# Attention through landmarks followed by an MLP: other buffers, another order of loads, and queries by parity of heads

## The chip, the core and the metric

The kernel runs on one core of a Trainium2 chip. A core has TensorE (PE: matmuls; PEld: its weight loads), VectorE (DVE), ScalarE (ACT), GpSimd (POOL) and SyncE (SP), which work beside each other and wait for one another by semaphores, a store SBUF, and PSUM, into which TensorE writes. [...] The metric is the device time of one execution in microseconds; lower is better.

## The reference

For each of 8 batches and 8 heads, with 576 tokens of 64 values and 32 landmarks:

```python
p_packed = sm_attn(p, k, v)            # softmax(scale * p k^T) v  : 32 x 64 per head
out      = sm_attn(q, p_packed, p_packed)   # 576 x 64 per head
x = out.transpose(0, 2, 1, 3).reshape(8 * 576, 512)
h = x @ w_in                           # 512 -> 2048
g = where(h >= 1, h, where(h <= -1, 0, (h + 1) ** 2 / 4))
return g @ w_out                       # 2048 -> 512, float32
```

Inputs are float32 and are drawn at random; the output is 4608 x 512 float32.

## The kernel before

All heads of a batch are worked on together, in bf16. Head h is G*a + g with G = 2, so g is its parity and a its pair. For each batch:

- The loads `k`, `q`, `v` (96 partitions, 8 heads, 6 x 64) are issued by POOL, which casts. The first four heads of batch 0's k, and batch 0's landmarks (`p_raw`), come as float32 by SP's and ACT's queues and are cast afterwards. The other batches' landmarks are one POOL load.
- `turned` (batches 0 and 1): TensorE transposes k and q head by head into `tp` in PSUM (line 362), VectorE and ScalarE copy them to `kT` and `qT`. `crossed` (batches from `FIRST` = 2): a DMA transpose on SP does it.
- `landmarks`: TensorE transposes p (`tpp`, line 321), four copies bring it to `pT`.
- `scores`: `sp` = kT by pT (line 413), exponential to `ex` (line 419). `packed`: `pk` = v by ex, with sums (lines 445, 450), to `ppT` and the scales `rs`.
- `probs`: `s` = ppT by qT (line 472), one PSUM tile for each parity g. Then for each g: exponential `eT` (482), sums `sm` (487), `ln` (491), `rc` = exp(-ln) (495), and on VectorE `A` = eT * rs * rc (500).
- The packed values are not multiplied out: `M` = w_in by ppT (`mp`, line 528, in four parts of 512 columns; then a copy) takes the place of w_in.
- `hidden`: for each of 16 slices fi of 128 hidden units, `h` = M by A (562); ScalarE makes `x` (567); VectorE or ScalarE the cut `t` (572, 574); VectorE `hT` = min(t, 1) * t (579).
- `output`: two batches are 9 tiles of 128 tokens; each is 16 matmuls `o` (619) over fi, a copy to `ob` and a store by SP (637).

PSUM has a pool `w` of three double banks for everything but outputs, and two banks for `o`.

The order on every engine is written out by a planner when the program is built. Each step is a `Task` with a rank, a price on each engine that may do it, what it depends on and which buffers it takes. `Plan.run` places the steps one after another in time, by its own prices, and the kernel is emitted in that order; the chip then runs each engine's list in order, with waits. Ranks come from constants at the top (`H1`, `T1`, `EARLY` and so on). Loads are a chain in the order of the list `LOADS`, of which at most eight are under way; a load also waits until the buffer that it fills is free. `BUFS` gives one buffer each to k and q, two to v. Finally, where the planner leaves TensorE free before the first output matmul, `warm` puts matmuls of zeros ("fillers", line 687), so that its clock stays up:

```python
n = math.ceil((t.start - at) / 0.2135) if at < 5.0 else int((t.start - at - 0.1) / 0.1085)
...
for w in [FW] * (n // 2) + [FW // 2] * (n % 2):
    nc.tensor.matmul(o[:, :w], zeros[:, :P], zeros[:, :w], start=True, stop=True)
```

How many fillers there are is fixed when the program is built.

Of the kernel before, what the change touches and what calls it, by code (L numbers as in the profile page):

```python
# [116 lines left out]
def kernel(  # L117
# [11 lines left out]
    f32 = mybir.dt.float32  # L129
    bf16 = mybir.dt.bfloat16  # L130
# [3 lines left out]
    B, H, S, D = q.shape  # L134
# [21 lines left out]
    PITCH0, PITCH1 = 1.03, 0.66  # L156
    T1, T2 = 3.22, 22.00
    LENT = [1, 4, 8]
    L1, M1 = 11.28, 4.03
    KT1, QT1 = 7.75, 9.62  # L160
    SC1, PK1 = 10.75, 9.34
    ST1, MT1 = 13.56, 16.34
    EARLY = [[(3.51, 23.7), (10.45, 10.36), (23.64, 1.0), (31.73, 16.65)], [(32.99, 9.77), (42.87, 11.2), (54.6, 5.54), (55.23, 18.49), (57.85, 4.06)]]

    V, A_, G_ = nc.vector, nc.scalar, nc.gpsimd
    nc.scalar.preload_act_table_set("natural_log_exp_and_others")

    BUFS = dict(w=3, o=2, k=1, q=1, v=2, kT=2, qT=2, ex=2, ppT=2, M=2, A=2, eT=4, ln=2, rc=2, x=4, t=4, ob=4)
    const = ctx.enter_context(tc.tile_pool(name="const", bufs=1))
# [48 lines left out]
    def constants(e):  # L218
        V.memset(zeros, 0.0)  # L219
        V.memset(pT[:, 0].rearrange("p g a x n -> p (g a x n)"), 0.0)  # L220
# [6 lines left out]
    consts = plan.add(-1000, {"DVE": (2.2, 2.2, constants)})  # L227

# [13 lines left out]
    def dma(key, rank, emit, mb, takes=(), settle=0.9):  # L242
# [6 lines left out]
        return t  # L249

    def tokens(nm, b):
        if (nm, b) not in have:
            have[nm, b] = new(nm, [TP, H, NC, D], bf16)
        return have[nm, b].rearrange("p h c d -> p h (c d)")

    def rows_of(nm, b, h0, h1):
        return {"k": k, "q": q, "v": v}[nm][b, h0:h1].rearrange("h (p c) d -> p h (c d)", c=NC)

    def load(nm, b, rank):

        parts = {("k", 0): [4, 8], ("q", 0): [0, 4, 6, 8]}.get((nm, b), [0, 8])
        for i, (h0, h1) in enumerate(zip(parts, parts[1:])):
            def emit(e, h0=h0, h1=h1):
                G_.dma_start(tokens(nm, b)[:, h0:h1], rows_of(nm, b, h0, h1))  # L264
            mb = MB0.get((nm, b, h0), 1.18 * (h1 - h0) / H)
            t = dma((nm, b, h0), rank + 0.01 * i, emit, mb, [nm] if i == 0 else [], 0.9 if b < 3 else 3.0)
            for h in range(h0, h1):
                landed[nm, b, h] = [t]
# [8 lines left out]
    def load_p(rank):  # L277
        dma("p", rank, lambda e: G_.dma_start(p_nat[:, 1:].rearrange("n b h d -> n (b h) d"),
                                              p[1:].rearrange("b h n d -> n (b h) d")), 0.6)

# [13 lines left out]
    def load_p_raw(e):  # L294
        for i, queue in enumerate((nc.sync, nc.scalar)):
            queue.dma_start(p_raw[:, 4 * i:4 * i + 4], p[0, 4 * i:4 * i + 4].rearrange("h n d -> n h d"))

    p_first = plan.add(-1000, {"SP": (1.0, 3.3, load_p_raw)})

    def load_k_raw(e):  # L300
        for i, queue in enumerate((nc.sync, nc.scalar)):
            queue.dma_start(k_raw[:, 2 * i:2 * i + 2], rows_of("k", 0, 2 * i, 2 * i + 2))

# [32 lines left out]

    p_cast = plan.add(-900, {"DVE": (0.41, 0.41, lambda e: V.tensor_copy(p_nat[:, 0], p_raw))}, [p_first])
    landmarks(0, 1, -900, [p_cast, identity])

    A_of, M_of, rs_of = {}, {}, {}  # L340

    def attention(b, at, fine):

        ready = {}

        def turned(nm, h0, h1):

            n = h1 - h0
            rank = at[nm + "T"] + 0.075 * h0
            banks = [(0, (0, 2)), (1, (2, 3))] if n == 4 else [(j, (0, E)) for j in range(n)]  # L350

            def place(tp, j, c):
                return tp[:, 0, (j * 2 + c) * TP:][:, :TP] if n == 4 and c < 2 else \
                    tp[:, 1, j * TP:][:, :TP] if n == 4 else tp[:, j, c * TP:][:, :TP]

            def turn(e):
                if h0 == 0:
                    have[nm + "T", b] = new(nm + "T", [P, H, E, TP], bf16)
                have["tp" + nm, b, h0] = tp = wide([P, 2, 1024], bf16, "tp")
                for c in range(E):  # L360
                    for j in range(n):
                        nc.tensor.transpose(place(tp, j, c),  # L362
                                            have[nm, b][:, h0 + j, X * c:X * (c + 1)].rearrange("p c d -> p (c d)"),
                                            ident[:TP, :TP])

            t = plan.add(rank, {"PE": (0.51 * n / 4, 0.17 + 0.51 * n / 4, turn)}, landed[nm, b, h0] + [identity],
                         ["w"] + ([nm + "T"] if h0 == 0 else []), behind=[ready.get((nm, "turn"))])
            ready[nm, "turn"] = t
            ev = []
            for y, (c0, c1) in banks:  # L370
                to = lambda y=y, c0=c0, c1=c1: (have[nm + "T", b][:, h0:h1, c0:c1] if n == 4 else
                                                have[nm + "T", b][:, h0 + y])
# [8 lines left out]
            for h in range(h0, h1):  # L381
                ready[nm, h] = ev
            return t

        def crossed(nm):
            def turn(e):
                have[nm + "T", b] = T = new(nm + "T", [P, H, E, TP], bf16)
                nc.sync.dma_start_transpose(T.rearrange("p h e t -> p (h e) t"),
                                            have[nm, b].rearrange("p h c d -> p (h c d)"))
            t = plan.add(at[nm + "T"], {"SP": (3.5, 11.0 if b < 4 else 6.5, turn)}, landed[nm, b, 0], [nm + "T"])  # L390
            chain("crossed", t)
# [5 lines left out]
        for nm in "kq":  # L397
            parts = [0, 4, 6, 8] if (nm, b) == ("q", 0) else [0, 4, 8]
            users[nm] = [turned(nm, *p) for p in zip(parts, parts[1:])] if b < FIRST else crossed(nm)
            plan.release(nm, users[nm])  # L400

# [28 lines left out]
        if b == 0:  # L430
            have["others"] = plan.add(-27, {"DVE": (1.56, 1.56, lambda e: V.memset(
                pT[:, 1:].rearrange("p b g a x n -> p (b g a x n)"), 0.0))}, [consts], behind=ready["k", 4])

# [31 lines left out]

        def probs(e):
            for g in range(G):
                have["s2", b, g] = s2 = wide([P, X, FW], f32, "s2")
# [6 lines left out]

        s2 = plan.add(at["s2"], {"PE": (0.32, 0.47, probs)}, pp + list({id(t): t for h in range(H) for t in ready["q", h]}.values()), ["w", "w", "eT", "eT"], mode="s")
        plan.release("qT", [s2])
        before = None
        for g in range(G):
# [23 lines left out]
            r = at["sm"] + 0.2 * g  # L503
            t_e = plan.add(r, {"ACT": (0.68, 0.745, exp)}, [s2, rs])
            plan.release("w", [t_e])
# [13 lines left out]
        for fs in groups:  # L519
# [28 lines left out]
        plan.release("ppT", mms + [s2])  # L548

# [173 lines left out]
```

## Time and profile before

| what | value |
| --- | --- |
| median of 3 runs | 249.87 us (249.86 to 250.2) |
| the profiled execution | 250.52 us |
| its span, first to last instruction | 248.7 us |
| busy: PE, PEld | 239.0, 136.7 us |
| busy: DVE, ACT, POOL | 176.9, 194.2, 27.9 us |
| granted TensorE clock | 1.000 |

A row of the timeline gives start, time taken, engine, line, operation, what is written and read, the number of instructions that were merged, and in brackets idle time of the engine ahead of it with what ended that. Of rows "who waited for whom" the numbers are total, times and longest. A busy TensorE is not one at its peak, since ends of matmuls are modelled; the starts of neighbours tell its pace. "DMA to landing" counts from the start of the issuing instruction.

### The profile page before, as it was taken

How to read it: one execution, taken by the hardware profiler on the slowest of the kernel's cores; microseconds unless marked ns; L12 is line 12 of the kernel's file. 1: busy time of each engine (PE TensorE's matmuls, PEld its weight loads, DVE VectorE, ACT ScalarE, POOL GpSimd, SP SyncE). 2: the span in 40 equal slices, each digit the busy share in tenths (PEclk: the TensorE clock that was granted, in tenths of full speed). 3: DMA queues.
4: the chain of work that ended last, by engine and by line, in shares of the span. 5: the costliest groups of instructions: out<-in, count | busy, mean ns of one | idle time of the engine just before them, and what ended most of it. 6: DMA issues, size and time to landing. Idle time of an engine off the chain costs nothing.

```text
span 248.7 us, 5748 instructions
## 1 busy us (share of the span) xinstructions
PE 239.0 (96%) x2330; PEld 136.7 (55%) x2368; DVE 176.9 (71%) x294; ACT 194.2 (78%) x320; POOL 27.9 (11%) x41
## 2 busy tenths in 40 slices
PE   7999999999999999999999999999999999999993
PEld 2645665456555664664556455655564555555453
DVE  4549997469937998897976796878976676776000
ACT  3587896889878999989997988799668978886111
POOL 8542100300110030021003000300000000000000
PEclk9999999999999999999999999999999999999999
DMA  7999999399999999799997979894941111122223
GB/s 153 189 206 207 200 199 194 58 228 196 179 169 223 173 164 214 123 180 175 195 147 150 202 160 176 154 204 110 171 105 45 42 45 42 43 46 77 59 75 84
DMA packets 59179, 35.83 MB, mean 144 GB/s; under 512 B 31888, under 2 KB 54672, under 8 KB 59152
## 3 DMA queue, kind: packets, MB, share of 16 engines
q0 software_dynamic: 24496, 18.29, 50.2%
q1 hardware_dynamic: 34080, 16.65, 32.2%
q10 hardware_dynamic: 576, 0.52, 0.7%
q8 instruction: 18, 0.29, 0.5%
q14 instruction: 9, 0.07, 0.1%
HBM read 37.22 MB, written 9.44 MB: 188 GB/s over the span
## 4 chain that ended last, share of the span: by engine, by line
PE 81%; DMA 8%; DVE 4%; ACT 2%; issue 2%; POOL 1%; POOLq 0%
PE o L619 44%; PE h L562 22%; DMA kT<-k 5%; DMA q<-in_q_dram 3%; PE mp L528 3%; DVE hT L579 2%; PE pk L445 2%; PE sp L413 2%; PE o L687 2%; PE sm L487 2%; PE s L472 1%; PE tp L362 1%; DVE t L572 1%; PE pk L450 1%; ACT x L567 1%
## 5 line engine op out<-in xcount | busy, mean ns | idle before, releaser
L619 PE MATMUL o<-w_out_sb,hT 128*128 128x512 bf16 (+1 forms) x557 | 142.3, 373 | 2.1 <-issue 0.5
L579 DVE SCALAR_TENSOR_TENSOR hT<-t 128x576 bf16<-128x576 f32 x128 | 95.1, 756 | 13.6 <-ACT t L574 11.1
L567 ACT ACTIVATE x<-h 128x576 f32<-128x576 f32 x128 | 80.3, 657 | 14.5 <-PE h L562 12.4
L562 PE MATMUL h<-A,M 128*128 128x288 bf16 x512 | 80.8, 286 | 0.8 <-DVE A L500 0.3
L619 PEld LDWEIGHTS <-hT 128*128 128x128 bf16 x592 | 56.0, 98 | 46.3 <-issue 4.5
L562 PEld LDWEIGHTS <-M 128*128 128x128 bf16 x512 | 49.4, 98 | 31.2 <-issue 2.6
L572 DVE TENSOR_SCALAR t<-x 128x576 f32<-128x576 f32 x72 | 33.6, 467 | 10.7 <-ACT x L567 10.2
L574 ACT ACTIVATE t<-x 128x576 f32<-128x576 f32 x56 | 38.5, 690 | 1.0
L189 ACT COPY ob<-o 128x512 f32<-128x512 f32 (+1 forms) x21 | 11.9, 568 | 15.7 <-PE o L619 15.7
L189 DVE CAST M<-mp 128x1024 bf16<-128x1024 f32 (+1 forms) x14 | 16.6, 1183 | 8.3 <-PE mp L528 8.2
L189 ACT CAST M<-mp 128x1024 bf16<-128x1024 f32 (+1 forms) x19 | 18.5, 994 | 2.2 <-PE mp L528 2.2
L264 POOL DMA_DIRECT2D q<-in_q_dram x10 | 7.3, 735 | 105.8 <-DMA qT<-q 82.0
L500 DVE SCALAR_TENSOR_TENSOR A<-eT,rs,rc 128x576 bf16<-128x576 bf16 x16 | 12.3, 812 | 3.5 <-ACT rc L495 3.5
L189 DVE COPY ob<-o 128x512 f32<-128x512 f32 x16 | 11.0, 689 | 5.3 <-PE o L619 4.8
L419 ACT ACTIVATE ex<-sp 96x768 bf16<-96x768 f32 x16 | 12.1, 801 | 2.9 <-PE sp L413 2.9
L687 PE MATMUL o<-zeros 128*128 128x512 bf16 (+1 forms) x45 | 12.6, 398 | 1.4 <-DVE zeros L219 1.2
L482 ACT ACTIVATE eT<-s,rs 128x576 bf16<-128x576 f32 x16 | 11.0, 737 | 1.0 <-DVE t L572 0.5
L491 ACT ACTIVATE ln<-sm 128x576 f32<-128x576 f32 x16 | 10.3, 652 | 0.5 <-PE sm L487 0.2
L189 ACT CAST ppT<-pk 64x128 bf16<-64x128 f32 x18 | 4.7, 259 | 7.6 <-PE pk L450 7.3
L528 PE MATMUL mp<-w_in_sb,ppT 64*32 64x512 bf16 x256 | 10.4, 382 | 0.0
L495 ACT ACTIVATE rc<-ln 128x576 f32<-128x576 f32 x16 | 10.0, 679 | 0.0
L413 PEld LDWEIGHTS <-kT 128*128 128x128 bf16 x192 | 7.3, 100 | 3.2 <-DMA kT<-k 0.7
(47 smaller groups left out, 108.5 us busy)
## 6 DMA issues: line engine op xcount, KB each, us to landing
v<-in_v_dram POOLq DMA_DIRECT2D x8, 576.0 KB, 10.0
out_dram<-ob SPq DMA_DIRECT2D x23, 192.0 KB, 2.4
k<-in_k_dram POOLq DMA_DIRECT2D x7, 576.0 KB, 11.9
q<-in_q_dram POOLq DMA_DIRECT2D x7, 576.0 KB, 6.9
out_dram<-ob SPq DMA_DIRECT2D x24, 128.0 KB, 2.4
w_in_sb<-in_moe_w_in_dram POOLq DMA_DIRECT2D x4, 512.0 KB, 13.1
w_out_sb<-in_moe_w_out_dram POOLq DMA_DIRECT2D x4, 512.0 KB, 18.3
out_dram<-ob SPq DMA_DIRECT2D x23, 64.0 KB, 2.0
```

The source lines that it names most:

```text
L189: i = (nc.vector.tensor_copy if e == "DVE" else nc.scalar.copy)(to, of)
L413: nc.tensor.matmul(o, kT[:, j * TP:j * TP + w], pT[:, b, g, 2 * i + a], start=True, stop=True)
L419: nc.scalar.activation(have["ex", b][:, :, 64 * i:64 * i + 64], have["sp", b, i][:TP, :E * X * G], AF.Exp, scale=scale)
L500: V.scalar_tensor_tensor(have["A", b][:, g], have["eT", b, g], rs_of[b][:, g, :1], have["rc", b, g], ALU.mult, ALU.mult)
L528: nc.tensor.matmul(mp[a * NP:(a + 1) * NP, g], have["ppT", b][r, g, a], w_in_sb[r, a, f * FW:(f + 1) * FW], start=True, stop=True)
L562: nc.tensor.matmul(h[:, hf, :HALF], M[:, g, fi * P:(fi + 1) * P], A[:, g, hf], start=(g == 0), stop=(g == G - 1))
L567: nc.scalar.activation(x, have["h", b, fi][:, :, :HALF], AF.Prelu, bias=-1.0, alpha=0.5)
L572: V.tensor_scalar(t, have["x", b, fi], 1.0, 0.0, ALU.add, ALU.max)
L574: nc.scalar.activation(t, have["x", b, fi], AF.Relu, bias=1.0)
L579: V.scalar_tensor_tensor(dst, t, 1.0, t, ALU.min, ALU.mult)
L619: nc.tensor.matmul(have["o", key][:, :w], hT[:, fi, i * P:(i + 1) * P], w_out_sb[:, fi, cols], start=(fi == 0), stop=(fi == KF - 1))
L687: nc.tensor.matmul(o[:, :w], zeros[:, :P], zeros[:, :w], start=True, stop=True)
```

## The change

It has four parts, and the planner's constants are set anew with them.

1. Batch 1's q gets a buffer of its own, `q1`, in the place of `k_raw`, which is free once batch 0's k has been cast; `p_raw` becomes a tile named `k1`, used by it alone. Batch 2's q then needs only batch 0's q to be transposed.
2. `LOADS`: batch 1's v comes ahead of the last two parts of w_out, the landmarks move behind batch 1's q, w_out's first part ahead of w_in's third, batch 2's v ahead of its q and k.
3. Batch 0's q is loaded and transposed in three parts by parity: heads 0 2 4 6, then 1 3, then 5 7 (before: 0 to 3, 4 5, 6 7). `probs` is two steps in batch 0, one for each parity, so the even half needs only the first part. Which engine makes the copies of the first part is fixed, and so is ScalarE for the first half of M's first part.
4. Landmarks of batches 0 and 1 come together by SP's and ACT's queues (one batch each) and are transposed together; the POOL load has six batches instead of seven, and their transposes come at batch 2's rank.

```diff
-    LOADS = "k0 v0 q0 win0 win1 win2 wout0 win3 wout1 k1 p wout2 v1 wout3 q1 q2 k2 v2"
-    H1, H2 = 18.20, 43.17
-    T1, T2 = 3.22, 22.00
+    Q0 = [range(0, 8, 2), range(1, 5, 2), range(5, 9, 2)]
+    LOADS = "k0 v0 q0 win0 win1 wout0 win2 win3 wout1 k1 v1 wout2 wout3 q1 v2 p q2 k2"
+    H1, H2 = 20.58, 43.72
+    T1, T2 = 1.70, 16.92
...
-    BUFS = dict(w=3, o=2, k=1, q=1, v=2, ...)
+    BUFS = dict(w=3, o=2, k=1, q=1, q1=1, v=2, ...)
...
-    p_raw = const.tile([NP, H, D], f32, name="p_raw")
+    p_raw = work.tile([NP, 2, H, D], f32, tag="k1", name="p_raw", bufs=1)
-    k_raw = const.tile([TP, 4, NC * D], f32, name="k_raw")
+    k_raw = work.tile([TP, 4, NC * D], f32, tag="q1", name="k_raw", bufs=1)
...
+    def home(nm, b):
+        return "q1" if (nm, b) == ("q", 1) else nm
...
-            queue.dma_start(p_raw[:, 4 * i:4 * i + 4], p[0, 4 * i:4 * i + 4].rearrange("h n d -> n h d"))
+            queue.dma_start(p_raw[:, i], p[i].rearrange("h n d -> n h d"))
...
-    landmarks(0, 1, -900, [p_cast, identity])
+    landmarks(0, 2, -900, [p_cast, identity])
...
+            if (nm, b, n) == ("q", 0, 4):
+                del ev[0].ways["ACT"], ev[1].ways["DVE"]
...
-            parts = [0, 4, 6, 8] if (nm, b) == ("q", 0) else [0, 4, 8]
+            parts = Q0 if (nm, b) == ("q", 0) else [range(4), range(4, 8)]
...
-        s2 = plan.add(at["s2"], {"PE": (0.32, 0.47, probs)}, pp + [every part of q], ["w", "w", "eT", "eT"], mode="s")
+        for gs in [[0], [1]] if fine else [[0, 1]]:
+            needs = {id(t): t for g in gs for h in range(g, H, G) for t in ready["q", h]}
+            t = plan.add(at["s2"] + 0.01 * gs[0], {"PE": (...)}, [pp of gs] + list(needs.values()), ["w", "eT"] * len(gs), mode="s")
...
-                    behind=[A_of[b][0]] if i else []) for i in range(n)]
+                    behind=[A_of[b][i]] if n > 1 and i else []) for i in range(n)]
+                if n > 1:
+                    del ms[0].ways["DVE"]
...
-        if b == 1:
-            landmarks(1, B, L1, [landed["p"], identity])
+        if b == 2:
+            landmarks(2, B, L1, [landed["p"], identity])
```

More of the change, by code (lines that the diff above doesn't have):

```diff
@@ L219, in constants @@
         V.memset(zeros, 0.0)
-        V.memset(pT[:, 0].rearrange("p g a x n -> p (g a x n)"), 0.0)
+        V.memset(pT[:, :2].rearrange("p b g a x n -> p (b g a x n)"), 0.0)
         V.memset(onesblk, 0.0)
@@ L249, in dma, with heads, rows_of, emit @@
         return t
+    def home(nm, b):
+        return "q1" if (nm, b) == ("q", 1) else nm
     def tokens(nm, b):
         if (nm, b) not in have:
-            have[nm, b] = new(nm, [TP, H, NC, D], bf16)
+            have[nm, b] = new(home(nm, b), [TP, H, NC, D], bf16)
         return have[nm, b].rearrange("p h c d -> p h (c d)")
-    def rows_of(nm, b, h0, h1):
-        return {"k": k, "q": q, "v": v}[nm][b, h0:h1].rearrange("h (p c) d -> p h (c d)", c=NC)
+    def heads(hs):
+        return slice(hs[0], hs[-1] + 1, hs.step)
+    def rows_of(nm, b, hs):
+        return {"k": k, "q": q, "v": v}[nm][b, heads(hs)].rearrange("h (p c) d -> p h (c d)", c=NC)
     def load(nm, b, rank):
[L261 to L267, printed above, removed]
+        for i, hs in enumerate({("k", 0): [range(4, 8)], ("q", 0): Q0}.get((nm, b), [range(H)])):
+            def emit(e, hs=hs):
+                G_.dma_start(tokens(nm, b)[:, heads(hs)], rows_of(nm, b, hs))
+            mb = MB0.get((nm, b, hs[0]), (1.3 if b == 2 else 1.18) * len(hs) / H)
+            t = dma((nm, b, hs[0]), rank + 0.01 * i, emit, mb, [home(nm, b)] if i == 0 else [], 0.9 if b < 2 else 1.5 if b == 2 else 3.0)
+            for h in hs:
                 landed[nm, b, h] = [t]
@@ L301, in load_k_raw @@
         for i, queue in enumerate((nc.sync, nc.scalar)):
-            queue.dma_start(k_raw[:, 2 * i:2 * i + 2], rows_of("k", 0, 2 * i, 2 * i + 2))
+            queue.dma_start(k_raw[:, 2 * i:2 * i + 2], rows_of("k", 0, range(2 * i, 2 * i + 2)))
     k_first = plan.add(-999, {"SP": (1.0, 4.3, load_k_raw)}, behind=[p_first])
@@ L430, in attention @@
         if b == 0:
-            have["others"] = plan.add(-27, {"DVE": (1.56, 1.56, lambda e: V.memset(
-                pT[:, 1:].rearrange("p b g a x n -> p (b g a x n)"), 0.0))}, [consts], behind=ready["k", 4])
+            have["others"] = plan.add(-27, {"DVE": (1.3, 1.3, lambda e: V.memset(
+                pT[:, 2:].rearrange("p b g a x n -> p (b g a x n)"), 0.0))}, [consts], behind=ready["k", 4])
         plan.release("kT", [scores(0), scores(1)])
@@ L464, in attention, with probs @@
         plan.release("w", pp + [rs])
-        def probs(e):
-            for g in range(G):
+        def probs(gs):
+            for g in gs:
                 have["s2", b, g] = s2 = wide([P, X, FW], f32, "s2")
@@ L474, in probs @@
                                          start=True, stop=True)
-        s2 = plan.add(at["s2"], {"PE": (0.32, 0.47, probs)}, pp + list({id(t): t for h in range(H) for t in ready["q", h]}.values()), ["w", "w", "eT", "eT"], mode="s")
-        plan.release("qT", [s2])
+        s2 = {}
+        for gs in [[0], [1]] if fine else [[0, 1]]:
+            needs = {id(t): t for g in gs for h in range(g, H, G) for t in ready["q", h]}
+            t = plan.add(at["s2"] + 0.01 * gs[0], {"PE": (0.08 + 0.12 * len(gs), 0.23 + 0.12 * len(gs), lambda e, gs=gs: probs(gs))},
+                         (pp if len(gs) > 1 else [pp[gs[0]]]) + list(needs.values()), ["w", "eT"] * len(gs), mode="s")
+            s2.update({g: t for g in gs})
+        plan.release("qT", list(set(s2.values())))
         before = None
@@ L547, in attention @@
                     M_of[b, Q * f + j] = ms[j * n // Q]
-        plan.release("ppT", mms + [s2])
+        plan.release("ppT", mms + list(set(s2.values())))
     g_of, h_of = {}, defaultdict(list)
```

48 lines of the change are left out of this document (24 added, 24 removed).

## The prediction

> **What bounds the kernel now.** I read the page first (its busy times, the chain that ended last, the groups), then the busy time of each engine by stretches, then the timeline of the opening and of the places where TensorE waits.
>
> ```profile
> PE 239.0 (96%) x2330; PEld 136.7 (55%) x2368; DVE 176.9 (71%) x294; ACT 194.2 (78%) x320; POOL 27.9 (11%) x41
> ...
> PE 81%; DMA 8%; DVE 4%; ACT 2%; issue 2%; POOL 1%; POOLq 0%
> ...
> L687 PE MATMUL o<-zeros 128*128 128x512 bf16 (+1 forms) x45 | 12.6, 398 | 1.4 <-DVE zeros L219 1.2
> ```
>
> TensorE is busy 96% of the span and holds 81% of the chain. But line 687 is filler: matmuls of zeros that `warm` puts where the planner leaves TensorE free before the first output matmul. So the time is: filler, plus useful matmuls, plus waits. The diff does not alter the useful matmuls; it can act only through the first and the last.
>
> ```profile
> 20.00:25.00 5.00, 4.61 (x36) 2.59 (x35) 4.80 (x8) 4.75 (x8) 0.76 (x1) 1.00 1.24 207
> ...
> 170.00:200.00 30.00, 29.61 (x284) 17.06 (x287) 24.06 (x39) 24.93 (x41) 0.00 (x0) 1.00 0.42 85
> ```
>
> Columns: stretch, its length, then busy PE, PEld, DVE, ACT, POOL, the granted clock, DMA share, GB/s. In the later stretch TensorE is full and the others have room. In the stretch from 20 us VectorE and ScalarE are both full (4.80 and 4.75 of 5.00): there batch 0's hidden layer runs as fast as they drain it. Ahead of that the loads set the pace. So the kernel is an opening bound by loads, then by ScalarE and VectorE, then TensorE to the end.
>
> **The fillers.** The order of the built program has 35 fillers of 512 columns and 6 of 256, against 40 and 8 before. A 512-column matmul advances by 0.216 us:
>
> ```profile
> 35.92 1.24 PE L619 MATMUL o<-w_out_sb,hT 128*128 128x512 bf16 x5
> ```
>
> (1.24 less 0.38 for the last one's own length, over four steps.) A half one costs 0.108. That is 5 x 0.216 + 2 x 0.108 = 1.30 us less for TensorE to do: **-1.30**, and all of it stays only if TensorE does not wait instead. The rest goes through the places where it could.
>
> **The opening chain to batch 0's first hidden matmul.**
>
> ```profile
> 13.30 0.43 PE L362 MATMUL tp<-ident,q 96*128 96x96 bf16 x6
> 13.77 0.40 ACT L189 COPY qT<-tp 128x288 bf16<-128x288 bf16 x1 [0.35 <-PE tp L362]
> 14.21 0.44 PE L472 MATMUL s<-qT,ppT 64*32 64x288 bf16 x16
> 14.60 1.37 ACT L482 ACTIVATE eT<-s,rs 128x576 bf16<-128x576 f32 x2 [0.43 <-PE s L472]
> 17.00 1.25 ACT L495 ACTIVATE rc<-ln 128x576 f32<-128x576 f32 x2
> 17.05 0.69 DVE L189 CAST M<-mp 128x512 bf16<-128x512 f32 x1 [2.97 <-PE mp L528]
> 17.71 1.55 DVE L500 SCALAR_TENSOR_TENSOR A<-eT,rs,rc 128x576 bf16<-128x576 bf16 x2
> 19.51 1.15 PE L562 MATMUL h<-A,M 128*128 128x288 bf16 x8
> 24.61 0.38 PE L619 MATMUL o<-w_out_sb,hT 128*128 128x512 bf16 x1 [0.35 <-DVE t L572]
> ```
>
> The queries' last part (13.30) starts a chain without a gap: its copy, the scores s, two exponentials, two logarithms, two reciprocals, A, h. With parity, the odd heads alone depend on the last part. But in the new TensorE order the first half of s stands behind the last transposes, and on ScalarE its exponential stands behind the last copy. So parity saves only the hop from copy to s to exponential: eT could start where the copy ends (14.17) instead of 14.60, **0.43 earlier**. Against that, both queues now load two batches' landmarks ahead of k_raw: 256 packets of 256 bytes more.
>
> ```profile
> q10 hardware_dynamic: 144, 0.03, 12.2%
> ```
>
> This is ScalarE's queue in the stretch 1.20 to 2.45: 12.2% of 16 engines for 1.25 us, over 144 packets, is 17 ns each. 256 x 17 ns over 16 engines is **+0.27** for everything behind, if the engines have no gap there; 0 if they have. I take 0.27, the worse end, since no row shows me such a gap. The chain thus gains 0.16. VectorE's first copy of M, which held A back until 17.71 although the first rc was done at about 17.62, goes to ScalarE and no longer stands there: bounds 0 to -0.09. First h: about 19.35 instead of 19.51. It is bound by data, so part of the filler cut ahead of it turns into waiting.
>
> What else the opening gains or loses I cost at **0**, by this cover:
>
> ```profile
> 5.63 0.56 DVE L189 CAST k<-k_raw 96x768 bf16<-96x768 f32 x1 [0.81 <-DMA k_raw<-in_k_dram]
> ```
>
> VectorE stands idle 0.81 ahead of k's cast. Ahead of it now stand a memset, a cast and copies of landmarks of twice the size, some 0.6 by the lengths of the old ones; and four transposes more on TensorE. k's chain itself ends before v has landed. The number of issuing instructions on SP and ScalarE is the same. Both halves of M's first part now run on ScalarE (0.6 more), in its idle 1.49 ahead of the first x (20.21, below). Splitting the scores adds no instruction. With all covers gone this is +0.3.
>
> From there the first output matmul: six h blocks, of which the sixth needs the PSUM buffer that the third x frees. x0 can start at 20.0 (h plus its latency); with one cut t behind it and x at 0.6 apart (1.19 for two), x2 ends near 22.5 and the first o starts at 23.1. It was 24.61 and waited 0.35 for VectorE. The new order has one mp block (0.41) fewer ahead of it, so at equal work this is 23.5 against 24.6: 1.1 of the 1.30 is kept, **+0.2** is lost in the opening (bounds 0 and 0.6, the latter if the x chain slips by one more cut).
>
> **ScalarE and VectorE up to the last h of batch 0.**
>
> ```profile
> 20.21 1.19 ACT L567 ACTIVATE x<-h 128x576 f32<-128x576 f32 x2 [1.49 <-PE h L562]
> 35.31 1.81 ACT L189 COPY pT<-tpp 64x896 bf16<-64x896 bf16 x2 [0.32 <-PE tpp L321]
> 39.33 0.65 ACT L567 ACTIVATE x<-h 128x576 f32<-128x576 f32 x1
> ```
>
> ScalarE takes 19.1 us from the first x to the sixteenth. The new order moves the landmark copies (1.81) out of this stretch, behind the reciprocals of batch 1, where ScalarE waits for A and h before it can go on, and brings in one cut (0.68) and batch 1's ppT copies (0.53): 0.6 us less work, starting 0.2 earlier. TensorE asks for the last h about 1 us earlier. I cost this at **0**; if the cover is gone it is up to +0.5.
>
> **Loads of batch 1.**
>
> ```profile
> 13.20 0.79 POOL L264 DMA_DIRECT2D k<-in_k_dram  x1 [0.32 <-PE tp L362]
> DMA to landing us min/median/max: 18.7/18.7/18.7
> ...
> 13.98 0.98 POOL L278 DMA_DIRECT2D p_nat<-in_p_dram  x1
> DMA to landing us min/median/max: 19.3/19.3/19.3
> ...
> 25.04 0.78 POOL L264 DMA_DIRECT2D q<-in_q_dram  x1 [2.73 <-DMA w_out_sb<-in_moe_w_out_dram]
> DMA to landing us min/median/max: 19.2/19.2/19.2
> 32.65 0.68 PE L362 MATMUL tp<-ident,k 96*128 96x96 bf16 x12
> 46.90 0.77 POOL L264 DMA_DIRECT2D q<-in_q_dram  x1 [21.08 <-PE o L619]
> ```
>
> (The landing rows are those of the k, landmark and q issues above them.) Batch 1's k lands at 13.20 + 18.7 = 31.9, the landmarks at 33.3, q at 44.2. The new list puts the landmarks behind q, so q comes 1.4 earlier, less the 0.27: 43.1. k comes at 32.2. The new program wants k's transposes after 8.4 us of matmuls and 0.5 of switches from the first o: 32.0, so **+0.15**. It wants q's 9.5 us of matmuls and 0.9 of switches later: 42.6 against 43.1, **+0.5** (bounds 0, without the 0.27 and with slower switches, and 1.0). GpSimd's wait of 21 us for batch 1's transposes goes, since batch 2's q no longer shares that buffer; this is what removes the pause in the loads.
>
> **Batch 1's A.**
>
> ```profile
> 46.97 0.71 PE L472 MATMUL s<-qT,ppT 64*32 64x288 bf16 x16
> 50.90 1.55 DVE L500 SCALAR_TENSOR_TENSOR A<-eT,rs,rc 128x576 bf16<-128x576 bf16 x2 [3.10 <-ACT rc L495]
> 51.77 0.42 PE L562 MATMUL h<-A,M 128*128 128x288 bf16 x2
> 52.50 2.88 PE L562 MATMUL h<-A,M 128*128 128x288 bf16 x22 [0.31 <-DVE A L500]
> 55.21 0.38 PE L619 MATMUL o<-w_out_sb,hT 128*128 128x512 bf16 x1
> ```
>
> 24 h matmuls of 0.1225 are 2.94 us; they took 55.21 - 51.77 = 3.44. So 0.5 was lost to A, which ended 5.5 us after s began. The new order has 24 landmark transposes and more output matmuls between s and h, 1.2 us of work, so A is ready first: **-0.5** (bounds 0 and -0.7).
>
> **Batches 2 and 3.**
>
> ```profile
> DMA to landing us min/median/max: 6.2/9.0/11.9
> ...
> 58.30 4.08 SPq L388 DMA_TRANSPOSE kT<-k  x1
> 73.72 6.89 SPq L388 DMA_TRANSPOSE kT<-k  x1
> ...
> PEld L413 <- DMA kT<-k: 0.7, 1, 0.7
> ```
>
> Batch 3's crossing (73.72, 11.9 to landing) made TensorE wait 0.7 on the weight side. Batch 2's (58.30) landed after 6.2. Batch 2's loads now run on from q's landing at 43.1, not from an issue at 46.90, but v and the landmarks stand ahead of q and k: the two q and k took 11.4 from issue to crossing; the 3.8 won less the landmarks' 1.4 is 2.4 earlier, if v costs only the start-up that is saved; so batch 2's crossing starts near 56 (bounds 53.5 and 58.3). Batch 3's k is loaded only after it, and so also comes about 2.4 earlier. On SP batch 3's two crossings now pass two stores, which wait behind them; of the four ob buffers three would then be full. TensorE wants batch 3's kT 1.9 earlier: 1.0 from the sum so far and 0.9 because its matmuls stand that much further ahead in the new order. So it is just in time: **-0.4** of the 0.7 (bounds -0.7, and +1.9 if the crossing does not come earlier at all).
>
> **Sum:** -1.30 + 0.2 + 0 + 0.15 + 0.5 - 0.5 - 0.4 = -1.35. The profiled execution took 250.52 (span 248.7 and 1.8 around it): 249.2. The median of the runs shown, 249.87, is 0.65 lower, so I take the difference to it: **248.5 us**. All the good ends together give 247.1 (-1.30 - 0.1 - 0.7 - 0.7); the bad ends of the opening and of batch 1 together (0.6 + 0.3 + 0.5 + 0.15 + 1.0, no gain from A) give 251.1.
>
> **Rivals.** *Loads no earlier* (chance 0.11): q of batch 1 still lands at 44.2, plus 0.27. Then TensorE stands 1.9 before its transposes instead of 0.5, and the sum is 249.9: no change. For it speaks that the stretch shares its DMA engines with the weights; against it that these are queued without gaps and the landmarks' 1.4 us stand in the rows.
>
> *Batch 2's crossing becomes the wait* (slower, 0.14).
>
> ```profile
> 66.50 0.73 PE sp L413 x24
> ```
>
> TensorE used batch 2's kT at 66.5; the new order wants it 1.35 of matmuls earlier, and 1.0 from the sum: near 64.2. With issue at 56 and 6.2 to land it is there at 62. If it takes batch 3's 11.9, because it meets other traffic, it lands at 68 and TensorE stands 3.7: 252.2. It decides from a landing after 65.6. Against it: no further load can follow batch 2's k until this crossing is done, so only stores run beside it.
>
> *A cold clock* (slower, 0.03). Fillers are thinner while TensorE waits.
>
> ```profile
> 1.19 2.95 PE L687 MATMUL o<-zeros 128*128 128x512 bf16 x7 [1.19 <-DVE zeros L219]
> 4.27 1.36 PE L687 MATMUL o<-zeros 128*128 128x512 bf16 x6
> ```
>
> The first seven fillers advance by about 0.42 each, twice the 0.216, though the clock column says 1.00; the later ones do not. Such a spell of 4 us in the hidden layer would cost 2 us: 250.5. The longest wait that I foresee is 0.5. [...]
>
> *The diff does not do what it says*: parity indeed brings little, as the order shows, and is priced so.
>
> **Numbers.** Forecast case 0.72 (247.5 to 249.3), no change 0.11, slower 0.17. A difference of 0.2% (0.5 us) is about what a measurement can tell. Faster 0.73, same 0.11, slower 0.16. The range, 247.5 to 250.1, takes in the no-change case.
>
> **What would show it.** Right: first h near 19.35 and first o near 23.1; q's transposes of batch 1 near 43.1; no gap in the first h block of batch 1; no wait for kT at batch 3. Wrong: first h later than 19.9, those transposes after 44.5, or a wait for kT in batch 2.

## The result, and the profile after

| | before | after |
| --- | --- | --- |
| median, first comparison | 249.95 us | 249.03 us (248.73 to 249.28), ratio 0.996 [0.9947, 0.9973] |
| median, second comparison (below, x0_after_again) | 250.09 us | 248.84 us (248.38 to 249.26), ratio 0.9948 [0.9931, 0.9965] |
| profiled execution (span) | 250.52 us (248.7) | 248.84 us (247.0); in the second comparison 248.63 (246.9) |

The change gains 0.9 to 1.3 us. First the profile page after: busy times, and the chain that ended last.

```profile
PE 237.7 (96%) x2324; PEld 136.4 (55%) x2361; DVE 175.0 (71%) x288; ACT 196.3 (79%) x326; POOL 27.8 (11%) x41
...
PE 88%; ACT 4%; DMA 3%; issue 2%; POOL 1%; POOLq 0%
```

TensorE is busy 1.3 us less, which is the filler, and now holds 88% of the chain instead of 81%. DMA fell from 8% to 3%. The page splits the chain by line as well, here before and then after:

```profile
PE o L619 44%; PE h L562 22%; DMA kT<-k 5%; DMA q<-in_q_dram 3%; PE mp L528 3%; DVE hT L579 2%; PE pk L445 2%; PE sp L413 2%; PE o L687 2%; PE sm L487 2%; PE s L472 1%; PE tp L362 1%; DVE t L572 1%; PE pk L450 1%; ACT x L567 1%
```

```profile
PE o L637 49%; PE h L580 25%; PE mp L543 4%; DMA q<-in_q_dram 3%; PE pk L455 2%; PE sp L423 2%; PE sm L502 2%; PE o L705 2%; ACT x L585 1%; PE s L482 1%; PE pk L460 1%; PE tp L369 1%; ACT ex L429 1%; ACT t L592 1%; ACT M L190 0%
```

The 5% of `kT<-k`, which is batch 3's transfer (73.72 to 85.59), is gone; the 3% of batch 0's q in the opening is still there. Next TensorE's timeline after (start, time taken, line, operation, instructions, idle time ahead with its releaser).

```profile
13.24 0.43 PE L369 MATMUL tp<-ident,q 96*128 96x96 bf16 x6
...
18.71 0.65 PE L580 MATMUL h<-A,M 128*128 128x288 bf16 x4
...
21.35 1.63 PE L580 MATMUL h<-A,M 128*128 128x288 bf16 x12 [0.35 <-ACT x L585]
22.82 0.38 PE L637 MATMUL o<-w_out_sb,hT 128*128 128x512 bf16 x1
...
27.67 0.39 PE L637 MATMUL o<-w_out_sb,hT 128*128 128x512 bf16 x1
28.87 1.20 PE L580 MATMUL h<-A,M 128*128 128x288 bf16 x8 [0.81 <-ACT M L190]
...
32.93 0.68 PE L369 MATMUL tp<-ident,k 96*128 96x96 bf16 x12
...
43.52 1.22 PE L369 MATMUL tp<-ident,q 96*128 96x96 bf16 x24
...
51.30 3.84 PE L580 MATMUL h<-A,M 128*128 128x288 bf16 x28
...
83.39 0.90 PE L423 MATMUL sp<-pT,kT 128*128 128x64 bf16 x24
...
237.67 5.60 PE L637 MATMUL o<-w_out_sb,hT 128*128 128x512 bf16 x41
```

The first h comes 0.80 earlier than before (19.51), the first o 1.79 earlier (24.61). Batch 1's h block (51.30) and batch 3's sp (83.39) have no wait in front. One wait is new: 0.81 at 28.87. The last row shows the end result. Before, at the very same time:

```profile
237.67 7.33 PE L619 MATMUL o<-w_out_sb,hT 128*128 128x512 bf16 x49
```

49 output matmuls were left then, 41 are left now (the row merges two forms: in both kernels the last 32 are of 256 columns). The eight fewer are full ones, and 8 x 0.216 = 1.73 us is the difference between the two profiled executions (1.7 by their spans). The list of TensorE's waits after (total, times, longest):

```profile
PE o L705 <- DVE zeros L220: 1.2, 1, 1.2
PE h L580 <- ACT M L190: 0.8, 1, 0.8
PE o L637 <- issue: 0.6, 4, 0.2
PE h L580 <- ACT x L585: 0.3, 1, 0.3
```

Neither A nor kT is in it any more. On ScalarE, VectorE and the queues of GpSimd and SyncE (the landing rows belong to the issue above them):

```profile
13.70 0.40 ACT L190 COPY qT<-tp 128x288 bf16<-128x288 bf16 x1 [0.35 <-PE tp L369]
14.00 1.38 ACT L497 ACTIVATE eT<-s,rs 128x576 bf16<-128x576 f32 x2
...
17.12 1.55 DVE L515 SCALAR_TENSOR_TENSOR A<-eT,rs,rc 128x576 bf16<-128x576 bf16 x2 [3.11 <-ACT rc L510]
...
27.81 1.01 ACT L190 CAST M<-mp 128x1024 bf16<-128x1024 f32 x1 [0.67 <-PE mp L543]
28.72 0.66 ACT L585 ACTIVATE x<-h 128x576 f32<-128x576 f32 x1
...
49.95 1.55 DVE L515 SCALAR_TENSOR_TENSOR A<-eT,rs,rc 128x576 bf16<-128x576 bf16 x2
```

```profile
21.77 0.79 POOL L271 DMA_DIRECT2D q<-in_q_dram  x1 [1.84 <-DMA w_out_sb<-in_moe_w_out_dram]
DMA to landing us min/median/max: 21.2/21.2/21.2
...
72.68 3.63 SPq L398 DMA_TRANSPOSE kT<-k  x1
DMA to landing us min/median/max: 5.4/5.4/5.4
```

The exponentials follow the last copy without a gap (14.00; before 14.60). Batch 1's q lands at 21.77 + 21.2 = 43.0 (before 44.2), its A begins at 49.95 (before 50.90), and batch 3's kT lands at 72.68 + 5.4 = 78.1 (before 73.72 + 11.9 = 85.6).

### The profile page after: what moved, and what is told of

Same layout as the page of the kernel before. It is cut to its first block, busy times and chain, and to the rows that moved or that the text cites. A ratio compares the mean times of both kernels' runs of the same rounds, so it can differ in the third digit from the quotient of the medians.

```text
span 247.0 us, 5732 instructions
## 1 busy us (share of the span) xinstructions
PE 237.7 (96%) x2324; PEld 136.4 (55%) x2361; DVE 175.0 (71%) x288; ACT 196.3 (79%) x326; POOL 27.8 (11%) x41
## 4 chain that ended last, share of the span: by engine, by line
PE 88%; ACT 4%; DMA 3%; issue 2%; POOL 1%; POOLq 0%
PE o L637 49%; PE h L580 25%; PE mp L543 4%; DMA q<-in_q_dram 3%; PE pk L455 2%; PE sp L423 2%; PE sm L502 2%; PE o L705 2%; ACT x L585 1%; PE s L482 1%; PE pk L460 1%; PE tp L369 1%; ACT ex L429 1%; ACT t L592 1%; ACT M L190 0%
## 5 line engine op out<-in xcount | busy, mean ns | idle before, releaser
L592 ACT ACTIVATE t<-x 128x576 f32<-128x576 f32 x60 | 41.4, 692 | 1.2
L590 DVE TENSOR_SCALAR t<-x 128x576 f32<-128x576 f32 x68 | 31.2, 459 | 12.2 <-ACT x L585 11.6
L190 ACT COPY ob<-o 128x512 f32<-128x512 f32 (+1 forms) x19 | 10.7, 565 | 15.1 <-PE o L637 15.1
L190 ACT CAST M<-mp 128x1024 bf16<-128x1024 f32 (+1 forms) x20 | 19.0, 975 | 3.0 <-PE mp L543 3.0
L190 DVE CAST M<-mp 128x1024 bf16<-128x1024 f32 x13 | 15.9, 1222 | 3.7 <-PE mp L543 3.6
L190 DVE COPY ob<-o 128x512 f32<-128x512 f32 x18 | 12.4, 690 | 5.3 <-PE o L637 4.9
L705 PE MATMUL o<-zeros 128*128 128x512 bf16 (+1 forms) x38 | 11.4, 421 | 1.4 <-DVE zeros L220 1.2
L510 ACT ACTIVATE rc<-ln 128x576 f32<-128x576 f32 x16 | 10.2, 685 | 0.0
L190 ACT CAST ppT<-pk 64x128 bf16<-64x128 f32 x20 | 5.2, 259 | 6.1 <-PE pk L460 5.8
L271 POOL DMA_DIRECT2D k<-in_k_dram x8 | 6.3, 792 | 30.8 <-DMA kT<-k 24.9
```

The source lines that it names most:

```text
L190: i = (nc.vector.tensor_copy if e == "DVE" else nc.scalar.copy)(to, of)
L271: G_.dma_start(tokens(nm, b)[:, heads(hs)], rows_of(nm, b, hs))
L590: V.tensor_scalar(t, have["x", b, fi], 1.0, 0.0, ALU.add, ALU.max)
L592: nc.scalar.activation(t, have["x", b, fi], AF.Relu, bias=1.0)
```

## The experiments

Each ratio is to the kernel before, on the same chip. x1, x2, x3 and x7 ran together, x4, x5, x6 and x8 together (before: 250.18 in both), and x0, x9, x10, x11 together (before: 250.09). After itself stands only in the last group, as x0, so the others are set against it through their ratios to before.

### The fillers: six back, and none at all

```diff
+    fill[-1] = fill[-1][0], fill[-1][1] + 12      # x1_fill_back: six of 512 columns more, in the last gap
```

> The changed kernel with six fillers of 512 columns put back (1.30 us of TensorE work, as much as the change took out), all in the last group of fillers, ahead of the third hidden block of batch 0; the order of all other work is the same. Theory A, the prediction's: a filler is TensorE time at its full price, so +1.30 against the changed kernel (about 250.3). Theory B: the fillers ahead of the first output matmul only fill waits, because in the changed kernel TensorE waits 0.35 there for ScalarE and 0.81 at 28.87 for ScalarE's copy of M, and both swallow what comes before: +0.2 to +0.6.

Measured: 249.89, ratio 0.999 [0.998, 1.0001], profiled span 247.6. TensorE's timeline:

```profile
20.38 1.67 PE L706 MATMUL o<-zeros 128*128 128x512 bf16 x7
21.89 1.63 PE L580 MATMUL h<-A,M 128*128 128x288 bf16 x12
23.36 0.38 PE L637 MATMUL o<-w_out_sb,hT 128*128 128x512 bf16 x1
...
29.41 1.20 PE L580 MATMUL h<-A,M 128*128 128x288 bf16 x8 [0.81 <-ACT M L190]
```

The wait of 0.35 for x disappears under the fillers. The first o is 0.54 later than after, and everything behind stays 0.54 later, the wait of 0.81 unchanged. This execution's first h was early (18.46); from the first h to the first o it took 4.90 against 4.11, so 0.79. The medians say 0.6 to 1.0. So 1.30 us of filler at this place is worth 0.5 to 1.0, between the two theories: the 0.35 had covered a wait that comes up when the fillers go, and of the two waits that theory B named the 0.81 swallowed nothing.

```diff
+    fill = []                                     # x7_no_fill
```

> The changed kernel without any filler (41 fewer matmuls of zeros), all else in the same order. Theory A: fillers are TensorE work that nothing needs, and none of the time in the opening is TensorE's: 0 to -0.5. Theory B: without them TensorE runs at half pace (0.43 for 512 columns, as the first seven fillers show) through the opening and into the hidden layer, where its matmuls then are late: +1 to +3. [...]

Measured: 250.57, ratio 1.0021 [1.0009, 1.0033], slower than before, as theory B had it. The timeline, and the row of the stretch from 5 us (length, busy PE, PEld, DVE, ACT, POOL, granted clock, DMA share, GB/s):

```profile
6.23 2.23 PE L369 MATMUL tp<-ident,k 96*128 96x96 bf16 x24 [1.50 <-DVE k L190]
...
20.56 4.22 PE L580 MATMUL h<-A,M 128*128 128x288 bf16 x20
24.62 0.38 PE L637 MATMUL o<-w_out_sb,hT 128*128 128x512 bf16 x1
```

```profile
5.00:10.00 5.00, 3.73 (x48) 3.32 (x48) 2.90 (x6) 3.11 (x7) 3.77 (x6) 1.00 1.29 195
```

20 h matmuls take 4.06 to the next start, 0.203 each instead of 0.1225: they start 0.24 apart up to about 23.8 and 0.1225 apart from there. The o behind them is at 24.62 instead of 22.82. The clock column says 1.00 all the while. The first h is hardly late (18.90 against 18.71), though A begins 0.7 later (17.83 against 17.12): up to there the data rule for the most part, and 1.6 of the 1.8 arise between the first h and the first o, in the hidden layer. So all the fillers together earn 1.3 to 1.6 us, while six more than after has cost.

### The new wait: M's last quarter

In the plan after, ScalarE copies the last quarter of M at 27.81; TensorE has one output matmul to put between that quarter's matmuls (27.33) and the next h. The weights for that h were loaded already at 27.68, before the copy began, so it is not M's data that it lacks but, as I read it, the PSUM buffer that the copy empties.

```diff
+                if b == 0 and f == 3:             # x2_m3_dve: the last quarter's copy on VectorE; the plan is redone
+                    del ms[0].ways["ACT"]
```

> The changed kernel with the copy of the last quarter of batch 0's M given to VectorE (it stood on ScalarE, ahead of the x of hidden block 8, and TensorE waited 0.81 for it at 28.87). The planner moves some 57 matmuls between the third and the fourth quarter of M. Theory: the wait is ScalarE's order alone, and goes: -0.4 to -0.8 against the changed kernel (248.2 to 248.6). Rival: VectorE is as full as ScalarE in this stretch, so the wait comes back behind its hT: within 0.2.

```diff
-                n = 2 if b == 0 and f == 0 else 1
+                n = 2 if b == 0 and f in (0, 3) else 1   # x10_m3_split: half on ScalarE, half on VectorE
```

> The changed kernel with the copy of the last quarter of batch 0's M cut in two, one half on each of ScalarE and VectorE, so that the PSUM buffer comes free about 0.4 us sooner than from either alone. Theory: the wait of 0.81 behind ScalarE's copy shrinks to 0.3 or less and VectorE's (0.41 in the run with the whole copy on VectorE) does not come up: -0.4 to -0.8 against the changed kernel. Rival: both engines are full there, the hidden blocks behind wait instead: -0.2 to +0.2.

Measured: x2 248.81, ratio 0.995 [0.9937, 0.9964], span 246.7; x10 249.36, 0.9963 [0.9949, 0.9978], span 247.7. The rows of x2 and then of x10 at that place:

```profile
29.04 1.14 PE L582 MATMUL h<-A,M 128*128 128x288 bf16 x8 [0.41 <-DVE M L190]
```

```profile
29.23 1.14 PE L582 MATMUL h<-A,M 128*128 128x288 bf16 x8 [0.94 <-ACT x L587]
```

On VectorE half the wait is left, and the span is 0.3 shorter; the medians cannot tell it from after. Both have 41 fillers by TensorE's weight loads (the trace of after lacks three of their matmul records), but the plan was redone and moved other matmuls too, so what the copy's place alone is worth is not separated. Split over both engines, the wait only changes its name: it ends with the x behind the half copy (28.53, 0.66 long). x10's opening ran 0.2 to 0.4 late as well, so its time proves nothing on its own.

### The buffer q1: taken away, and given alone

```diff
-        return "q1" if (nm, b) == ("q", 1) else nm
+        return nm                                 # x3_no_q1; k_raw then has a place of its own
```

> The changed kernel with batch 1's q in the common q buffer again; TensorE's order is the same, but batch 2's q cannot be loaded before batch 1's transposes (43.3 to 44.5). Theory A: the own buffer is what takes the wait for batch 3's kT away (0.6 us of TensorE's lag): +0.4 to +0.7. Theory B: the new list puts batch 2's v and the landmarks between batch 1's and batch 2's q, and these keep the DMA engines at work until about 46.9; the buffer adds nothing: within 0.2.

Measured: 249.56, ratio 0.9974 [0.9964, 0.9985], span 248.4. Its queues and TensorE:

```profile
44.90 0.77 POOL L271 DMA_DIRECT2D q<-in_q_dram  x1 [17.29 <-PE tp L369]
...
72.31 7.05 SPq L398 DMA_TRANSPOSE kT<-k  x1
...
101.00 2.91 SPq L398 DMA_TRANSPOSE kT<-k  x1
DMA to landing us min/median/max: 6.4/6.4/6.4
```

```profile
107.48 0.54 PE L423 MATMUL sp<-pT,kT 128*128 128x64 bf16 x12 [0.82 <-DMA kT<-k]
```

The pause of 17.29 is back, and the crossing of batch 3 takes 7.05 on SyncE instead of 3.63. But the wait does not come at batch 3: its sp is at 83.24 with no wait. The late crossing makes batch 4's loads late, batch 4's kT is issued at 101.00 instead of 96.60 and lands at 107.4, and there TensorE waits, 0.82 on the matmul side and 1.3 on the weight side. Opening and batch 1 are those of after; the whole loss of the span lies behind 83 us. But this profiled execution, 250.19, was the longest of its twelve: the medians lose only 0.3 to 0.6 against after, so a wait of 1.3 is not what most of them have.

```diff
-                  BUFS = dict(w=3, o=2, k=1, q=1, v=2, ...)
+                  BUFS = dict(w=3, o=2, k=1, q=1, q1=1, v=2, ...)   # x4_before_q1: the kernel before, k_raw and batch 1's q in q1
```

> The kernel before with one part of the change alone: batch 1's q in a buffer of its own, so that batch 2's q, k and v are loaded without the pause of 21 us. The planner moves its later work with it. Theory: the wait for batch 3's kT (0.4 to 0.6 of TensorE's lag) goes, the opening stays: -0.4 to -0.6 against the kernel before. Rival: earlier loads of batch 2 only meet the loads of batch 1 and the stores: within 0.2.

Measured: 249.82, ratio 0.9984 [0.9968, 1.0], span 248.0. Batch 3's kT, used at

```profile
80.00 0.53 PE L413 MATMUL sp<-pT,kT 128*128 128x64 bf16 x12
```

is waited for nowhere. The crossing itself still took 6.24 on SyncE, but it was issued at 68.36 instead of 73.72 and landed at 76.7. So the buffer alone brings 0.4 by the medians (the interval just reaches no gain), and without it after loses 0.3 to 0.6: the two agree, each close to what the intervals can tell.

### Parity: with the plan redone, and with every order kept

```diff
-    Q0 = [range(0, 8, 2), range(1, 5, 2), range(5, 9, 2)]
+    Q0 = [range(0, 4), range(4, 6), range(6, 8)]  # x5_no_parity
```

> The changed kernel with batch 0's q in contiguous parts again (heads 0 to 3, 4 5, 6 7), so both halves of the scores need the last part. The planner now sets 38 fillers of 512 and 5 of 256 (0.54 us more). Theory A (fillers at full price): +0.5. Theory B: the first exponential comes 0.4 to 0.6 later and with it the first hidden block, and most of this is swallowed by the wait of 0.81 at 28.87: 0 to +0.3.

Measured: 252.43, ratio 1.0078 [1.0052, 1.0103], slower than before. But the timeline shows where, and it isn't the opening:

```profile
52.04 0.40 PE L580 MATMUL h<-A,M 128*128 128x288 bf16 x2 [0.53 <-DVE A L515]
...
53.77 3.58 PE L580 MATMUL h<-A,M 128*128 128x288 bf16 x26 [1.33 <-DVE A L515]
```

The planner, with other dependencies at the start, wrote another order on ScalarE around batch 1's logarithms, and A of batch 1 came late. That is a price of the constants being set for one plan, not of parity. x9_parity_frozen therefore keeps every order and filler of after, maps the three parts back to heads 0 to 3, 4 5, 6 7 in load, transposes and copies, and moves only the even scores, with what hangs on them, behind the last qT copy, since they now need it.

> The changed kernel with batch 0's q in contiguous parts (heads 0 to 3, 4 5, 6 7) and the order of every engine and the fillers as in the changed kernel: parity alone undone, not the plan. The first half of the scores then waits for the copies of the last part. Theory A: the first exponential and the first hidden block come 0.4 to 0.7 later, and the chain through ScalarE carries this on: +0.3 to +0.6 against the changed kernel. Theory B: what the planned-anew run without parity lost (3 us) was parity: +2 or more. Theory C: the later waits swallow it: within 0.2.

Measured: 249.17, ratio 0.9956 [0.9937, 0.9976], span 247.3; the unchanged kernel beside it 248.84, span 246.9. First x9, then the unchanged kernel:

```profile
14.20 1.37 ACT L505 ACTIVATE eT<-s,rs 128x576 bf16<-128x576 f32 x2 [0.30 <-PE s L488]
...
18.91 0.65 PE L588 MATMUL h<-A,M 128*128 128x288 bf16 x4
```

```profile
13.70 1.38 ACT L497 ACTIVATE eT<-s,rs 128x576 bf16<-128x576 f32 x2
...
18.52 0.65 PE L580 MATMUL h<-A,M 128*128 128x288 bf16 x4
```

The exponential comes 0.50 later, the first h 0.39, the span 0.4. Starts of single executions vary as much: with this opening unchanged the first h came at 18.46 (x1) to 18.94 (x10). The hop inside one execution is steadier: from the start of the last copy of q to the exponential it takes 0.69 in x9 (13.51 to 14.20) and 0.29 to 0.30 in after, x0, x2, x3, x6 and x10, so 0.39 is parity and the other 0.1 a later copy. The medians (0.3 apart) lean the same way, and their intervals overlap.

> The changed kernel as it is, once more, beside the three below. Both theories: 0.995 to 0.997 of the kernel before. If the profile shows a wait for kT of batch 4 as the run without the own q buffer did (1.2 us), that wait is a matter of the execution and not of the buffer; if it does not, the buffer keeps it away.

x0_after_again is after without an edit, for this comparison; its times stand in the table at the top. Its trace has no wait for kT at batch 4 or anywhere else.

### The landmarks: back ahead of v, and heavier

```diff
-    LOADS = "... wout1 k1 v1 wout2 wout3 q1 v2 p q2 k2"
+    LOADS = "... wout1 k1 p v1 wout2 wout3 q1 v2 q2 k2"   # x6_p_early
```

> The changed kernel with the other batches' landmarks back at their old place in the loads, ahead of batch 1's v, so batch 1's v and q land 1.3 to 1.4 us later (q near 43.9 to 44.2, where TensorE now begins its transposes at 43.3). Theory A: TensorE waits for q: +0.6 to +1.0. Theory B: batch 1's chain has room behind q, because the softmax ends ahead of its first hidden block, and output matmuls fill in: within 0.3.

Measured: 250.27, ratio 0.9995 [0.998, 1.001], span 248.8: all that the change gains is gone.

```profile
45.40 0.68 PE L369 MATMUL tp<-ident,q 96*128 96x96 bf16 x12
...
53.26 2.88 PE L580 MATMUL h<-A,M 128*128 128x288 bf16 x22 [0.30 <-DVE A L515]
```

q lands at 24.9 + 19.8 = 44.7, 1.7 later than in after: that is the price of the landmarks for the loads behind them (the prediction had put it at 1.4). The transposes of q come 1.9 later. Of that, 0.5 is there at the first o already (23.33), 0.7 is the 24 landmark transposes, which in this plan stand ahead of q's, and 0.42 and 0.15 are waits, of M's matmuls for batch 1's sums and of an output matmul for w_out. And with the landmark transposes gone from between s and h, the 0.30 for A is back, as the prediction's step on A argued. Theory A's wait for q is not among these, and the 0.5 in the opening is not shown to come from the landmarks: the planner wrote a new order here too, so x6 doesn't price their place alone.

```diff
-    p_raw = work.tile([NP, 2, H, D], ...)
+    p_raw = work.tile([NP, 2, H + 6, D], ...)     # x8_p_more: each queue loads 14 heads, 384 packets of 256 bytes more
...
-            queue.dma_start(p_raw[:, i], p[i].rearrange("h n d -> n h d"))
+            queue.dma_start(p_raw[:, i], p.rearrange("b h n d -> n (b h) d")[:, H * i:H * i + H + 6])
```

> The changed kernel with 14 heads of landmarks instead of 8 on each of the two queues ahead of k_raw: 384 packets of 256 bytes more, which nothing reads. Theory A, the prediction's: 17 ns each over 16 engines, +0.41 for everything behind, k_raw, v and q of batch 0: q 0.4 later, first hidden block 0.3 to 0.4 later. Theory B: the DMA engines have gaps before 4 us, so k_raw comes later but v and q do not: 0.

```diff
+    fill[0] = fill[0][0], fill[0][1] + 2          # x11_p_more_fill: x8, with one filler more in the first gap
```

> The changed kernel with 14 heads of landmarks on each queue ahead of k_raw, as before, and one filler of 512 columns more in the first group, which closes the gap of 0.46 us that TensorE had ahead of the landmark transposes (there its pace stayed at half until 9.8). Theory A: what the larger landmark load cost was the half pace after that gap; without the gap TensorE runs at full pace from about 5 us and the run comes within 0.3 of the changed kernel. Theory B: it was the 0.4 to 0.8 by which k_raw came later: still +0.5 to +1.

Measured: x8 250.08, ratio 0.9989 [0.9974, 1.0004]; x11 249.32, 0.9972 [0.9959, 0.9984], but its profiled execution, 250.42, was the longest of its twelve. Batch 0's q landed 8.4 after issue in x8 and 8.6 in x11 (after: 8.2; before: 8.5; the ten runs with after's landmark loads: 7.8 to 8.5), k_raw 5.0 in both (4.3; 4.5; 4.2 to 5.1), the landmarks 3.0 and 3.4 (2.4 in after). So the delay of q that theory A names is no larger than what executions differ by. What moved clearly is the landmarks and TensorE's pace. First x8, then x11:

```profile
4.82 0.39 PE L328 MATMUL tpp<-ident,p_nat 32*128 32x32 bf16 x8 [0.46 <-DVE p_nat L344]
5.14 2.31 PE L705 MATMUL o<-zeros 128*128 128x512 bf16 x5
7.25 2.12 PE L369 MATMUL tp<-ident,k 96*128 96x96 bf16 x24
```

```profile
5.31 0.39 PE L328 MATMUL tpp<-ident,p_nat 32*128 32x32 bf16 x8 [0.52 <-DVE p_nat L344]
5.63 2.31 PE L706 MATMUL o<-zeros 128*128 128x512 bf16 x5
```

The five fillers take 2.31 (after: 1.63) and 24 transposes 2.12 (after: 22 in 1.14); full pace comes only near 9.7. The first h was at 19.77 in x8. x1 tells the parts apart, since its five fillers also ran at half pace (2.29) and its first h came at 18.46: of the 1.31 between them, 0.52 is there at the landmarks' transposes (4.82 against 4.30), 0.51 is k's transposes at half pace (1.93 to the next start against 1.42), and the rest arises in the scores, which begin at half pace. So the pace is the larger part, but not all of it. In x7, which was at half pace all through this stretch but had no fillers to run, the first h came at 18.90. x11 was to close the gap of 0.46 and, in the execution that was profiled, didn't: one filler at half pace fills 0.43, and the landmarks came later still. Against before, x11's median is 0.7 better than x8's, but the execution that was profiled does not show why. Whether the gap decides the pace therefore stays open.

## Why the prediction was right, and where it was off

The number (248.5) lies 0.3 to 0.5 below the two medians, inside its range, and the forecast case is the one that happened. By its steps:

- **Fillers and opening** (-1.30 + 0.2). First o: 23.1 predicted, 22.82 measured, so by the same working (one mp block of 0.41 less ahead) 1.4 was won instead of 1.1. The first h was 0.64 earlier than predicted, 18.71 against 19.35. Of the 0.64, 0.33 is the landmarks' +0.27: the last transposes of q began at 13.24, not 0.27 behind 13.30 but 0.06 ahead of it. No delay shows here; with one opening q's landing varies from 7.8 to 8.5 after issue, so one execution could not show 0.27, and 384 packets more, an estimated 0.41 by the same working, went with 8.4 and 8.6. Parity gave 0.1 more than priced (from the last copy to the exponential 0.30 instead of 0.83, so 0.53 against 0.43; x9 shows 0.39). The remaining 0.21 I overlooked: the second mp block now stands behind the first four h instead of ahead of them, and from A to h it takes 1.59 instead of 1.80.
- **ScalarE and VectorE up to the last h of batch 0** (0, up to +0.5). This step failed. I added up ScalarE's work and found less of it; but TensorE lost 0.81 at 28.87 on a round trip, from mp through a copy of 1.01 to the next h, with one output matmul to put between. The busy time of an engine doesn't show that; the order of the two engines side by side would have.
- **k and q of batch 1** (+0.15, +0.5). The landings were right: k at 32.1 (32.2 predicted), q at 43.0 (43.1). The waits were not there, because TensorE, late by that same 0.81, asked at 32.93 and 43.52. The loss was one and came in another place. In x2, which keeps half of it, q's transposes began at 43.18 without a wait either.
- **A of batch 1** (-0.5). Right in mechanism: no wait in the block at 51.30. At the block's start TensorE has done the same useful work in both kernels by its weight loads, 64 of hT and 64 of M, and is 0.5 ahead of before (51.30 against 51.77). At its end it is 0.8 ahead (four h and one output matmul more done at 55.15 than before at 55.21), so the block itself gave 0.3 of the 0.5; predicted up to there were 0.95.
- **Batch 3's kT** (-0.4 of 0.7). Right in mechanism, too small: it was in place 5.3 us before its use, not just in time, since the crossing now meets less traffic: batch 3's v landed at 64.4 + 10.2 = 74.6 instead of 68.8 + 13.7 = 82.5. Batch 2's crossing was at 54.48 (56 predicted) and its use at 64.05 (64.2). x3 and x4 point to the buffer as the cause, and x3 shows that without it the wait appears a batch later than I had it. Of the 1.7 between the profiled executions, 0.9 arises behind batch 1, more than twice the 0.4.
- **From the profile to the median.** The sum -1.35 stands against -1.7 and -1.9 in the profiled executions, and -0.9 and -1.25 in the medians. The profiled execution of before, 250.52, was a long one (the medians beside the experiments were 249.95 to 250.18), those of after are 0.2 below their medians. I carried over the whole difference of 0.65, which was too much. So the close number is in part luck: a sum that was 0.35 to 0.55 too small for the profiled executions met a correction that was too large for the medians.
- **The rivals.** Loads no earlier: q landed at 43.0, so not the case; x6, where q lands at 44.7, comes out at no change, as that rival had it, but without the wait for q that it named. Batch 2's crossing: used at 64.05, landed at 60.2, far from deciding. The cold clock: no relapse in after, where behind the new wait of 0.81 the eight h matmuls took 1.04 from 28.87 to the next start, 0.13 each. That a longest wait of 0.5 speaks against it was my estimate; no run shows how long a wait would bring it on. x7 shows its price in the hidden layer: half pace from the first h at 18.90 to about 23.8, and a first o 1.8 later (predicted: 2 us for 4 us). But it was not a relapse, which is what I had looked for: without fillers TensorE had not yet reached full pace.

## What to carry to other kernels

Where an engine is full, follow each round trip through another engine (its matmul, the copy, the next matmul that needs the buffer) in the planned order; sums of busy time don't show what is late (here the 0.81 at 28.87). When one part of a planned kernel is undone, keep every other order and filler, or the new plan is what is measured (parity undone: 252.43 in x5, 249.17 in x9). A wait that a buffer causes may show up a batch later than the transfer that it delays (x3: a crossing of 7.05 for batch 3, a wait of 0.82 at batch 4), so look for it behind the place where it was priced.

## What the runs showed of the hardware that I had not expected

- **TensorE's pace is not in the clock column.** It read 1.00 in x7 while 24 transposes took 2.23 (after: 22 in 1.14) and h matmuls 0.203; the rows' pace tells, and it is this pace that the fillers keep up: with them h matmuls advanced by 0.1225 from the first on (18.71 in after). Without fillers half pace lasted to about 23.8, though TensorE was busy for 3.73, 4.80 and 3.00 of the three stretches of 5.00 from 5 us on. In kernels with the same opening the five fillers after the landmarks took 1.35, 1.63, 2.00 and 2.29 (x0, after, x10, x1): by the spacing of single fillers (0.43 at half pace, 0.216 at full) the switch came at about 4.8, 5.4, 6.2 and 6.8, so it moves from execution to execution by two microseconds. In x8, x11 and x7 it came about 5 us after TensorE's last wait ahead of it (9.7 after 4.82, 10.5 after 5.31, 23.8 after 18.90); three cases do not make a rule. What decides the point is not shown.
- **A DMA transpose took longer with loads beside it.** A kT crossing held SyncE for 2.8 to 4.0 us with no load of q, k or v beside it or less than 3 us of them. It held it for 4.1 to 4.5 beside 3.7 us or more of a v load alone (before and x4 at batch 2, x7 at batch 3), and for 6.2 to 7.05 beside a q and a v load (batch 3 of before, x3, x4, x5 and x6). To landing it took 5.0 to 7.0, 6.2 to 8.1 and 8.3 to 11.9.
- **What 256-byte packets cost the loads behind them stays open.** By the prediction's estimate of 17 ns each over 16 DMA engines, from the 144 packets in its row of ScalarE's queue, 384 more are 0.41 us. With them batch 0's q landed after 8.4 and 8.6 us (x8, x11), without them after 7.8 to 8.5 in ten runs: the spread is as large as the price.
